# The first pair of groups 1 and 2 from SBUF, and their first products in two chains

## The chip, the cores and the metric

The kernel runs on one core of one Trainium2 chip. The metric is the device time of one execution in microseconds, the median of several runs.

## The reference

Three stages follow each other on 1536 tokens of width 512: an attention over a window of 16 and over summaries of blocks of 32 keys, a gated feed-forward layer (part 1 here), and a second feed-forward layer (part 2), which is all that the change names:

```python
def _moe2_ref(x, w_in, w_out) -> np.ndarray:
    h = x @ w_in
    g = h - np.tanh(h)
    return (g @ w_out).astype(np.float32)
```

In part 2 `x` is 1536 x 512, `w_in` 512 x 2048 and `w_out` 2048 x 512, all float32.

## The kernel before

Each float32 operand is split into a high half (a cast to fp32r, on ScalarE) and a low half (the difference, on VectorE or GpSimd), and each product is three matmuls: high by high, high by low, low by high (`mm3`, lines 838 to 840). The tokens form three groups of 512. The 2048 hidden columns of part 2 form 16 blocks of 128, taken two at a time: eight pairs n = 0 to 7.

For a pair, `h` is computed in seven block products instead of eight (`product(k, ...)`, k = 1 to 7, six matmuls of 256 columns each), here called the first products. Sums of the products on VectorE give the four quarters of `h`; then come tanh (ScalarE) and `h - tanh(h)` (VectorE). For groups 0 and 1 the result is split into `hh` and `hl` and multiplied by two blocks of `w_out` straight away: the second products, eight of a pair, three matmuls of 512 columns each, which add up in four `acc` banks over the eight pairs. Group 2 keeps its results in `wd[1]`, and its second products come last, again in seven block products (`last_seconds`), pair after pair.

The blocks of weights of the seven first products are sums of quarters of `w_in`. Group 0 makes them (`make`): sums in `sm`, split into the tiles `ih` and `il` in the large buffer `mix` (`eh` and `el` for pair 0), and stores them in DRAM as `ki{n}` (line 1305, two tiles of 1024 and two of 768 columns). Groups 1 and 2 load them (`fetch`) into `l0` and `l1`, places in `wd[0]`. In the same way group 0 stores the out-weights `kd`, group 1 loads them into `th` tiles (`fetch_d`, line 1341; two tiles), splits them (`direct_outs`, ScalarE at line 1361) and makes the block sums for the last stage (`make_values`), which are stored as `kv{n}` and loaded again by `place_values`.

The order of every engine is found by a planner in the kernel: each operation has an engine, a duration, the operations that it follows, the buffers that it takes and a due time; the planner starts what is ready, most urgent first, and emits the instructions in that order. Operations marked `flex` go to VectorE or GpSimd; the function `yields` decides whether GpSimd leaves one to VectorE. `LAG`, `EASE` and `RID` shift due times. All first products follow each other in one chain, `chain["first"]`; the pairs of groups 1 and 2 are visited as (1,0), (1,1), (2,0), (2,1), (1,2), (2,2), ... Transfers go through SyncE's queue in the planned order.

Of the kernel before, what the change touches and what calls it, by code (L numbers as in the profile page):

```python
# [59 lines left out]
LAND = 1.0  # L60
LAG = 4.0
EASE = 24.0
RID = 2.0
HOLD = 1.0
FRONT = 0.0
FAR = 4.0
# [29 lines left out]
class Plan:  # L96
# [25 lines left out]
    def order(self, filler=None, gap=0.0):  # L122
# [39 lines left out]
        def yields(o, eng, now):  # L162

            return eng == "pool" and free.get("dve", 0.0) <= now + 0.3 and any(
                q.late < o.late and q.port and q.ready <= now + 1e-9 and can(q, now) for _, _, q in ready.get("dve", [])
            )
# [115 lines left out]
def kernel(  # L282
# [1091 lines left out]
    def fetch(n):  # L1374
        weights = {}
        at = 0
        for i, ks in enumerate(turns):
            m = len(ks) * q
            w = [slot(f"l{i}"), slot(f"l{i}")]
            o = dma_both(m, True, w, [k[:, at:at + m] for k in keep_i[n]], *stored[n], *after_a, *made_o)  # L1380
            for i, k in enumerate(ks):
                weights[k] = (*w, i * q, *o)
            at += m
        return weights

    def make(n):
# [36 lines left out]
        for ks, pieces in zip(  # L1423
# [22 lines left out]
            m = len(ks) * q  # L1446
            store += dma_both(m, False, (wh, wl), [k[:, at:at + m] for k in keep_i[n]], *[o for p in done for o in p])
            for i, k in enumerate(ks):
                weights[k] = (wh, wl, i * q, *done[i])
            at += m  # L1450
        after_a.extend([o1, o2, o3, o4] + [o for p in weights.values() for o in p[3:]])
        stored[n] = store
        return direct_outs(n), weights

    direct = []
    halves_of = {}
    kept = lambda f: wd[1][:, f * 512:(f + 1) * 512]

    def pair(g, n, at, weights=None, period=PAIR):
# [11 lines left out]
        def product(k, m, out, opens, *after, closes=True):  # L1471
            wh, wl, w0, a, z = weights[k]
            h, l = operand[g][k]

            def run():
                for c in range(2):
                    s = slice(w0 + c * P, w0 + (c + 1) * P)
                    mm3(out(), wh[:, s], wl[:, s], h()[:, c], l()[:, c], opens and c == 0, closes and c == 1)

            count[0] += 1  # L1480
            o = pe(0.71, run, chain.get("first"), a, z, *ready[g][k], *after, slots=[m, wh, wl], due=at + count[0] * (PAIR if g < 2 else OPS * 0.715) / OPS)
            chain["first"] = o
            second_first.setdefault(g, []).append(o)
            return o
# [75 lines left out]

        opens, closes = n == 0, n == NF2 // 2 - 1
        nt = GROUPS[g][1]
# [6 lines left out]
        for j in (1, 0):  # L1569
            oh, ol, do = outs[j]  # L1570
            for i in range(nt):
# [7 lines left out]
                if not (closes and j == 0):  # L1579
                    continue  # L1580
                ob = slot("th")
                m = DM // 2
                a = act(0.27, lambda i=i, ob=ob: nc.scalar.copy(ob[:, :m], ps[i][:, :m]), after2, slots=[ps[i], ob], due=due + RID)
                z = dve(0.33, lambda i=i, ob=ob: nc.vector.tensor_copy(ob[:, m:], ps[i][:, m:]), after2, slots=[ps[i], ob], due=due + RID)
                t0_ = GROUPS[g][0]
# [18 lines left out]
    def make_values(n, d, outs, ld):  # L1604
# [4 lines left out]
        def put(ks, w, z):  # L1609
            m, c = len(ks) * q, CUTS[ks[0]]  # L1610
            for i, k in enumerate(ks):
                done[k] = *w, i * q, *z
            if n + 1 < NF2 // 2:
                stored_v.setdefault(n, []).extend(dma_both(m, False, w, [k[:, c:c + m] for k in keep_v[n]], *z, due=due))

        def item(ks, j, *after):
            w = slot("vh"), slot("vl")
            gate = [o for k in stored for o in stored[k]]
            put(ks, w, cut(lambda: d[j][:], lambda: w[0][:], lambda: w[1][:], 2 * q, chain.get("v"), *after, *gate, slots=[d[j], *w]))

# [15 lines left out]
    def h_forms(n):  # L1636
# [7 lines left out]
        def make_item(ks, src, m, *after):  # L1644
            hi, lo = slot("fh"), slot("fl")
            gate = second_first[1] if n == 0 and ks[0] < 3 else second_first[2]
            a, z = cut(src, lambda: hi[:, :m], lambda: lo[:, :m], m, chain.get("f"), *after, *gate, slots=[hi, lo])
            chain["f"] = a
            for i, k in enumerate(ks):
                forms[k] = hi, lo, i * q, a, z  # L1650
            return a, z
# [17 lines left out]
    def place_values(n):  # L1669

        if n + 1 == NF2 // 2:
            return
# [15 lines left out]
    def last_seconds(n, at, opens, closes):  # L1688
# [9 lines left out]
        for k in (1, 6, 7, 5, 2, 3, 4) if opens or closes else (1, 2, 4, 6, 7, 3, 5):  # L1698
            fh, fl, f0, *fo = forms[k]
            vh, vl, v0, *vo = values[n][k]  # L1700
            for a in range(2):
# [6 lines left out]
                count += 1  # L1708
                ss = [fh, fl, ps[k]] + ([vh, vl] if n + 1 == NF2 // 2 else [])
                after2 = pe(0.358, run, after2, *fo, *vo, slots=ss, due=at + count * 0.358)  # L1710
# [102 lines left out]
    prepare(2, at + PAIR)  # L1813
    line = [(g, 2 * k + j) for k in range(n_all // 2) for j in range(2) for g in (1, 2)]
    line[1], line[2] = line[2], line[1]
    weights = {}
    v_due = {n: at + 2 * n * 7.7 + EASE for n in range(n_all)}
    for i, (g, n) in enumerate(line):
        if n not in weights:
            weights[n] = fetch(n)  # L1820
        pair(g, n, at, weights[n], 2 * 7.75)
        at += 7.75
    at += 4.0
    for n in range(n_all):
        ends = last_seconds(n, at, not n, n + 1 == n_all)
        at += 2 * OPS * 0.358
# [111 lines left out]
```

## Time and profile before

| | |
|---|---|
| median of 3 runs | 652.35 us (648.78 to 653.7) |
| profiled execution | 650.38 us |
| its span in the trace | 648.5 us |
| TensorE busy | 631.1 us, 97% |
| VectorE, ScalarE, GpSimd busy | 523.6, 398.1, 107.6 us |
| DMA moved | 126.60 MB |
| group 0 of part 2 ends, groups 1 and 2 begin | at about 467 us |
| last stage of group 2 begins | at about 604 us |

The span is the stretch between the first and the last instruction of the profiled execution; 1.9 us of that execution lie outside it. A row names the line of the kernel, the engine and the tiles: `mid` and `bank` are PSUM banks, `mix` and `wd` are the two large buffers in SBUF that hold weights, `pad`, `hi`, `lo`, `rest` and `raw` are buffers that change their use from stage to stage. Where a text speaks of a matmul's distance from the next, the starts are compared, since ends overlap.

### The profile page before, as it was taken

How to read it: one execution, taken by the hardware profiler on the slowest of the kernel's cores; microseconds unless marked ns; L12 is line 12 of the kernel's file. 1: busy time of each engine (PE TensorE's matmuls, PEld its weight loads, DVE VectorE, ACT ScalarE, POOL GpSimd, SP SyncE). 2: the span in 40 equal slices, each digit the busy share in tenths (PEclk: the TensorE clock that was granted, in tenths of full speed). 3: DMA queues.
4: the chain of work that ended last, by engine and by line, in shares of the span. 5: the costliest groups of instructions: out<-in, count | busy, mean ns of one | idle time of the engine just before them, and what ended most of it. 6: DMA issues, size and time to landing. Idle time of an engine off the chain costs nothing.

```text
span 648.5 us, 11072 instructions
## 1 busy us (share of the span) xinstructions
PE 631.1 (97%) x3786; PEld 547.0 (84%) x3786; DVE 523.6 (81%) x1130; ACT 398.1 (61%) x829; POOL 107.6 (17%) x165
## 2 busy tenths in 40 slices
PE   7999999999999999999999999999899999999997
PEld 6997778789887888887888888898799999999996
DVE  5789878988699977888988989978666776668785
ACT  3996678878676545546656767665555555556441
POOL 2212333223042020221200002311020101110000
PEclk9999999999999999999999999999999999999999
DMA  9989457889300000235323255566477988898731
GB/s 333 354 267 330 157 158 239 287 296 307 102 1 1 33 1 1 97 130 172 124 64 130 116 187 206 206 241 231 156 267 227 351 282 295 269 375 343 266 142 66
DMA packets 46625, 126.60 MB, mean 195 GB/s; under 512 B 5560, under 2 KB 10600, under 8 KB 46568
## 3 DMA queue, kind: packets, MB, share of 16 engines
q1 hardware_dynamic: 46568, 125.89, 55.4%
q8 instruction: 30, 0.49, 0.3%
q14 instruction: 27, 0.22, 0.1%
HBM read 91.00 MB, written 34.87 MB: 194 GB/s over the span
## 4 chain that ended last, share of the span: by engine, by line
PE 80%; DMA 8%; DVE 7%; ACT 3%; issue 1%; SPq 0%; POOL 0%; DVEq 0%; ACTq 0%
PE bank L838 15%; PE bank L840 14%; PE bank L839 14%; PE mid L838 10%; PE mid L840 10%; PE mid L839 10%; PE bank L674 2%; DMA pad<-in_units_dram 2%; PE bank L580 2%; DMA hi<-in_w_dram 1%; PE bank L685 1%; DMA wd<-in_ksum_dram 1%; DMA wd<-in_units_dram 1%; DMA raw<-in_w_dram 1%; PE bank L631 1%
## 5 line engine op out<-in xcount | busy, mean ns | idle before, releaser
L838 PE MATMUL mid<-hi,mix 128*128 128x512 f32 (+1 forms) x160 | 63.6, 398 | 0.0
L840 PE MATMUL mid<-hi,mix 128*128 128x512 f32 (+1 forms) x160 | 59.5, 372 | 0.0
L840 PE MATMUL bank<-mix,hl 128*128 128x512 f32 x128 | 50.7, 396 | 0.0
L838 PE MATMUL bank<-mix,hh 128*128 128x512 f32 x128 | 50.6, 395 | 0.0
L838 PE MATMUL bank<-hh,mix 128*128 128x512 f32 (+1 forms) x128 | 50.0, 390 | 0.6 <-ACT hh L856 0.3
L839 PE MATMUL bank<-mix,hh 128*128 128x512 f32 x128 | 50.4, 394 | 0.0
L814 ACT CAST mix<-wd 128x512 fp32r<-128x512 f32 x66 | 40.3, 619 | 16.1 <-PE bank L839 12.1
L839 PE MATMUL bank<-hl,mix 128*128 128x512 f32 (+1 forms) x128 | 48.6, 379 | 1.0 <-DVE hl L859 1.0
L840 PE MATMUL bank<-hh,mix 128*128 128x512 f32 (+1 forms) x128 | 48.3, 378 | 0.0
L816 DVE TENSOR_TENSOR mix<-wd,mix 128x512 fp32r<-128x512 f32 x59 | 40.2, 683 | 8.6 <-ACT mix L814 8.5
L839 PE MATMUL mid<-lo,mix 128*128 128x512 f32 (+1 forms) x112 | 40.6, 363 | 0.0
L608 ACT ACTIVATE pad<-pad,st 128x184 f32<-128x184 f32 x88 | 32.3, 438 | 7.0 <-DVE st L594 6.9
L840 PE MATMUL mid<-pad,mix 128*128 128x256 f32 (+1 forms) x104 | 34.9, 335 | 1.5 <-DVE mix L1058 1.5
L838 PEld LDWEIGHTS mid<-hi,mix 128*128 128x128 f32 x160 | 30.1, 188 | 6.8 <-issue 2.7
L838 PE MATMUL mid<-pad,mix 128*128 128x256 f32 (+1 forms) x104 | 35.1, 337 | 0.2 <-ACT rest L1499 0.2
L840 PEld LDWEIGHTS mid<-hi,mix 128*128 128x128 f32 x160 | 30.1, 188 | 5.8
L839 PE MATMUL mid<-pad,mix 128*128 128x256 f32 (+1 forms) x104 | 34.8, 335 | 0.0
L1107 ACT COPY lo<-mid 128x512 f32<-128x512 f32 x36 | 21.0, 586 | 22.0 <-PE mid L840 21.5
L1110 DVE TENSOR_TENSOR lo<-lo,bank 128x512 f32<-128x512 f32 x36 | 24.5, 684 | 8.8 <-ACT lo L1107 6.4
L840 PE MATMUL bank<-pad,mix 128*128 128x512 f32 (+1 forms) x90 | 30.8, 343 | 0.0
L839 PE MATMUL bank<-pad,mix 128*128 128x512 f32 (+1 forms) x90 | 30.8, 342 | 0.0
L838 PE MATMUL bank<-pad,mix 128*128 128x512 f32 (+1 forms) x90 | 30.8, 342 | 0.0
(343 smaller groups left out, 2053.7 us busy)
## 6 DMA issues: line engine op xcount, KB each, us to landing
raw<-in_w_dram SPq DMA_DIRECT2D x38, 512.0 KB, 4.9
kv<-mix SPq DMA_DIRECT2D x42, 256.0 KB, 3.9
pad<-in_units_dram SPq DMA_DIRECT2D x19, 442.0 KB, 5.5
hi<-in_w_dram SPq DMA_DIRECT2D x16, 512.0 KB, 5.3
wd<-ki SPq DMA_DIRECT2D x16, 512.0 KB, 5.6
wd<-in_w_dram SPq DMA_DIRECT2D x14, 512.0 KB, 4.6
ki<-mix SPq DMA_DIRECT2D x14, 512.0 KB, 3.8
wd<-ki SPq DMA_DIRECT2D x16, 384.0 KB, 6.6
```

The lines of the kernel that those rows point to most:

```text
L580: nc.tensor.matmul(ps[e][:, j * SC:(j + 1) * SC], q[r, j], k[r, j], start=(j == 0), stop=(j == NP - 1), skip_group_check=True,)
L608: nc.scalar.activation(s, s, AF.Exp, bias=st[:, 0, h:h + 1], scale=-1.0)
L631: nc.tensor.transpose(pt[:, h * P:(h + 1) * P], sc[:, m0:m0 + P], ident)
L674: nc.tensor.matmul(av[:, h * (D + 1):(h + 1) * (D + 1)], ph[:, h * P:(h + 1) * P], v[:, h], start=(h == 0), stop=False, skip_group_check=True,
L685: nc.tensor.matmul(av[:, 2 * j * (D + 1):2 * (j + 1) * (D + 1)], ph[0:TAIL + 1, (4 + j) * P:(5 + j) * P], vtn[0:TAIL + 1, j].rearrange("p ...
L814: a = act(0.52, lambda c=c: nc.scalar.copy(wh[:, c], d[:, c]), dep, chain.get(tag), slots=[wh])
L816: on.tensor_tensor(wl[:, c], d[:, c], r32(wh[:, c]), ALU.subtract)
L838: nc.tensor.matmul(o, ah, bh, start=first, stop=False, skip_group_check=True)
L839: nc.tensor.matmul(o, ah, bl, start=False, stop=False, skip_group_check=True)
L840: nc.tensor.matmul(o, al, bh, start=False, stop=last, skip_group_check=True)
L1107: return act(0.52, lambda: nc.scalar.copy(u[m][:], mx[m][:]), *after, *free, slots=[u[m], mx[m]])
L1110: return dve(0.62, lambda: nc.vector.tensor_tensor(u[m][:], u[m][:], my[m][:], ALU.add), *after, slots=[u[m], my[m]])
```

## The change

Pair 7, which group 0 does last, is not stored: `make` hands its split weights on in `carried`, and groups 1 and 2 do pair 7 first, from `ih` and `il` in `mix`. The pairs then go in the order `TURN` = 7, 0, 1, ..., 6, group 1 and group 2 by turns, and the last stage in the same order. Each group has its own chain of first products. Pair 6 is now the one whose out-weight sums stay in SBUF; those of pair 7 are cut into free places of `l0` and `l1` and stored as `kv7`, and the load of pair 1 waits for that. Group 1's results leave through `tb` tiles. The look-ahead in `yields` goes from 0.3 to 2.0, `LAG` from 4 to 2, `EASE` from 24 to 16.

```diff
-LAG = 4.0
-EASE = 24.0
+LAG = 2.0
+EASE = 16.0
+YIELD = 2.0
+RIG = 2.0
+OFF = 2.0
+BOTH = 15.5
+TURN = [NF2 // 2 - 1, *range(NF2 // 2 - 1)]
...
         def yields(o, eng, now):
 
-            return eng == "pool" and free.get("dve", 0.0) <= now + 0.3 and any(
+            return eng == "pool" and free.get("dve", 0.0) <= now + YIELD and any(
...
-            o = dma_both(m, True, w, [k[:, at:at + m] for k in keep_i[n]], *stored[n], *after_a, *made_o)
+            o = dma_both(m, True, w, [k[:, at:at + m] for k in keep_i[n]], *stored[n], *after_a, *made_o, *(stored_v[TURN[0]] if n == TURN[2] else []))
...
-            store += dma_both(m, False, (wh, wl), [k[:, at:at + m] for k in keep_i[n]], *[o for p in done for o in p])
+            if n != TURN[0]:
+                store += dma_both(m, False, (wh, wl), [k[:, at:at + m] for k in keep_i[n]], *[o for p in done for o in p])
...
         stored[n] = store
+        if n == TURN[0]:
+            carried[n] = weights
         return direct_outs(n), weights
...
-            o = pe(0.71, run, chain.get("first"), a, z, *ready[g][k], *after, slots=[m, wh, wl], due=at + count[0] * (PAIR if g < 2 else OPS * 0.715) / OPS)
-            chain["first"] = o
+            o = pe(0.71, run, chain.get(("first", g)), a, z, *ready[g][k], *after, slots=[m, wh, wl], due=at + count[0] * (BOTH if g else PAIR) / OPS)
+            chain["first", g] = o
...
-        opens, closes = n == 0, n == NF2 // 2 - 1
+        opens, closes = (n == 0, n == NF2 // 2 - 1) if not g else (n == TURN[0], n == TURN[-1])
...
-                ob = slot("th")
+                ob = slot("tb" if g else "th")
...
         def item(ks, j, *after):
-            w = slot("vh"), slot("vl")
-            gate = [o for k in stored for o in stored[k]]
-            put(ks, w, cut(lambda: d[j][:], lambda: w[0][:], lambda: w[1][:], 2 * q, chain.get("v"), *after, *gate, slots=[d[j], *w]))
+            if n == TURN[0]:
+                w = [slot(f"l{j}") for i in range(2)]
+                gate = after_a + made_o
+            else:
+                w = [slot("vh"), slot("vl")]
+                gate = [o for g in (1, 2) for o in second_first[g][:OPS]] + [o for k in stored for o in stored[k]]
+            put(ks, w, cut(lambda: d[j][:], lambda: w[0][:, :2 * q], lambda: w[1][:, :2 * q], 2 * q, chain.get("v"), *after, *gate, slots=[d[j], *w]))
...
-    line = [(g, 2 * k + j) for k in range(n_all // 2) for j in range(2) for g in (1, 2)]
-    line[1], line[2] = line[2], line[1]
-    weights = {}
-    v_due = {n: at + 2 * n * 7.7 + EASE for n in range(n_all)}
+    line = [(g, TURN[2 * k + j]) for k in range(n_all // 2) for j in range(2) for g in (1, 2)]
+    weights = carried
+    v_due = {n: at + i * BOTH + EASE for i, n in enumerate(TURN)}
     for i, (g, n) in enumerate(line):
         if n not in weights:
             weights[n] = fetch(n)
-        pair(g, n, at, weights[n], 2 * 7.75)
-        at += 7.75
+        pair(g, n, at + (OFF if g == 2 else 0.0), weights[n], BOTH)
+        at += BOTH / 2
     at += 4.0
-    for n in range(n_all):
-        ends = last_seconds(n, at, not n, n + 1 == n_all)
+    for n in TURN:
+        ends = last_seconds(n, at, n == TURN[0], n == TURN[-1])
```

First place: TensorE where group 1 begins. `mid<-hi` is the first product k = 1 of group 1, the rows with `hh` and `hl` are second products of pair 6 of group 0; `wd` holds loaded blocks, `mix` those that group 0 made. Before:

```order
L838 MATMUL bank_78<-mix_89,hh_94 128x512
L839 MATMUL bank_78<-mix_89,hh_94 128x512
L840 MATMUL bank_78<-mix_89,hl_96 128x512
L838 MATMUL mid_81<-hi_0_61,wd_1_4142 128x256
L839 MATMUL mid_81<-hi_0_61,wd_1_4142 128x256
L840 MATMUL mid_81<-hi_0_61,wd_1_4142 128x256
```

Now:

```order
L843 MATMUL bank_76<-mix_89,hh_94 128x512
L844 MATMUL bank_76<-mix_89,hh_94 128x512
L845 MATMUL bank_76<-mix_89,hl_96 128x512
L843 MATMUL mid_81<-hi_0_61,mix_89 128x256
L844 MATMUL mid_81<-hi_0_61,mix_89 128x256
L845 MATMUL mid_81<-hi_0_61,mix_89 128x256
```

And where, in the new order, the first matmul on a loaded block comes (the rows with `pad` are first products of group 2):

```order
L843 MATMUL mid_82<-pad_1942,mix_89 128x256
L844 MATMUL mid_82<-pad_1942,mix_89 128x256
L845 MATMUL mid_82<-pad_1942,mix_89 128x256
L843 MATMUL mid_81<-hi_0_61,wd_1_4134 128x256
L844 MATMUL mid_81<-hi_0_61,wd_1_4134 128x256
L845 MATMUL mid_81<-hi_0_61,wd_1_4134 128x256
```

One second product more stands ahead of group 1, and its first product that reads `wd` stands 84 matmuls behind its first product of all.

Second place: VectorE at what was 208 us of the trace. L1058 (now L1063) makes low cuts of weights in `mix`, L1110 and L1135 (L1115 and L1140) add the two halves of a sum and apply the gate. Before:

```order
L1110 TENSOR_TENSOR lo_0_65<-lo_0_65,bank_78 128x512
L1110 TENSOR_TENSOR lo_0_65<-lo_0_65,bank_76 128x512
L1135 SCALAR_TENSOR_TENSOR th_91<-th_91,lo_0_65 128x512
L1058 TENSOR_TENSOR mix_89<-lo_0_65,mix_89 128x512
L1136 TENSOR_TENSOR th_91<-th_91,lo_0_65 128x512
L1058 TENSOR_TENSOR mix_89<-rest_71,mix_89 128x512
```

Now:

```order
L1115 TENSOR_TENSOR lo_0_65<-lo_0_65,bank_78 128x512
L1063 TENSOR_TENSOR mix_89<-lo_0_65,mix_89 128x512
L1115 TENSOR_TENSOR lo_0_65<-lo_0_65,bank_76 128x512
L1063 TENSOR_TENSOR mix_89<-rest_71,mix_89 128x512
L1140 SCALAR_TENSOR_TENSOR th_91<-th_91,lo_0_65 128x512
L1063 TENSOR_TENSOR mix_89<-lo_0_65,mix_89 128x512
L1141 TENSOR_TENSOR th_91<-th_91,lo_0_65 128x512
```

The cut `mix<-lo` that stood behind both sums and the gate now stands between the two sums, and a second cut stands ahead of the gate.

Third place: SyncE's queue in the middle of groups 1 and 2. `kv<-mix` stores sums of out-weights, `th<-kd` loads out-weights, `wd<-ki` loads blocks of first products. Before:

```order
L1305 DMA wd_1_4142<-ki_0_104 128x1024
L1305 DMA wd_1_4142<-ki_1_105 128x1024
L1305 DMA kv_0_132<-mix_89 128x512
L1305 DMA kv_1_133<-mix_89 128x512
L1305 DMA kv_0_132<-mix_89 128x512
L1305 DMA kv_1_133<-mix_89 128x512
L1341 DMA th_92<-kd_119 128x512
L1341 DMA th_91<-kd_118 128x512
L1305 DMA wd_1_4142<-ki_0_104 128x768
L1305 DMA wd_1_4142<-ki_1_105 128x768
```

Now:

```order
L1310 DMA wd_1_4134<-ki_0_102 128x768
L1310 DMA wd_1_4134<-ki_1_103 128x768
L1310 DMA kv_0_132<-mix_89 128x512
L1310 DMA kv_1_133<-mix_89 128x512
L1310 DMA kv_0_132<-mix_89 128x512
L1310 DMA kv_1_133<-mix_89 128x512
L1346 DMA th_91<-kd_119 128x512
L1346 DMA th_92<-kd_118 128x512
L1310 DMA wd_1_4134<-ki_0_104 128x1024
L1310 DMA wd_1_4134<-ki_1_105 128x1024
```

The two loads `th<-kd` stand behind the last two pairs of stores `kv` as before; the second half of the loads `wd<-ki` now stands ahead of these stores.

## Rows read from the trace of the kernel before

**Rows 1.** The page, part 1: busy us, share of the span and instructions.

```profile
...
PE 631.1 (97%) x3786; PEld 547.0 (84%) x3786; DVE 523.6 (81%) x1130; ACT 398.1 (61%) x829; POOL 107.6 (17%) x165
...
```

**Rows 2.** The page, part 4: the chain that ended last, by engine.

```profile
...
PE 80%; DMA 8%; DVE 7%; ACT 3%; issue 1%; SPq 0%; POOL 0%; DVEq 0%; ACTq 0%
...
```

**Rows 3.** Busy us by stretch (x instructions), then granted clock, DMA share, GB/s.

```profile
...
455.00:475.00 20.00, 17.68 (x102) 15.55 (x101) 12.23 (x22) 10.15 (x22) 1.22 (x1) 0.91 0.59 214
475.00:500.00 25.00, 25.00 (x169) 23.01 (x168) 17.42 (x33) 14.16 (x34) 5.09 (x5) 1.00 0.65 225
500.00:525.00 25.00, 24.54 (x171) 22.79 (x171) 17.24 (x37) 13.94 (x31) 1.86 (x2) 1.00 0.94 337
525.00:600.00 75.00, 75.00 (x515) 69.50 (x514) 52.81 (x107) 41.71 (x92) 8.12 (x9) 1.00 0.85 310
...
```

**Rows 4.** TensorE's waits, whole span: us in total, times, longest.

```profile
...
PE mid L840 <- DVE mix L1058: 1.5, 1, 1.5
...
PE bank L839 <- DVE hl L859: 1.0, 2, 0.7
...
```

**Rows 5.** TensorE's waits from 440 to 648 us.

```profile
...
PE mid L838 <- DMA wd<-ki: 1.5, 1, 1.5
PE mid L840 <- DMA wd<-ki: 0.8, 1, 0.8
PE mid L838 <- ACT lo L1499: 0.5, 1, 0.5
PE bank L838 <- ACT th L1583: 0.3, 1, 0.3
```

**Rows 6.** Timeline of SyncE's queue at 465 us: start, us, what.

```profile
...
464.97 3.70 SPq L1305 DMA_DIRECT2D wd<-ki  x8
...
```

**Rows 7.** Timeline of TensorE at the same place.

```profile
...
466.39 0.39 PE L839 MATMUL bank<-mix,hh 128*128 128x512 f32 x1
466.62 0.39 PE L840 MATMUL bank<-mix,hl 128*128 128x512 f32 x1
468.54 0.39 PE L838 MATMUL mid<-hi,wd 128*128 128x256 f32 x1 [1.53 <-DMA wd<-ki]
...
469.83 0.49 PE L840 MATMUL mid<-hi,wd 128*128 128x256 f32 x1 [0.78 <-DMA wd<-ki]
...
```

**Rows 8.** One microsecond behind it, columns as in rows 3.

```profile
...
470.00:471.00 1.00, 1.00 (x5) 1.00 (x6) 0.00 (x0) 0.00 (x1) 0.00 (x0) 0.50 1.04 414
...
```

**Rows 9.** Groups of VectorE, then ScalarE, 480 to 600 us: busy, mean ns, idle before.

```profile
...
L1557 DVE TENSOR_TENSOR hl<-lo,hh 128x512 fp32r<-128x512 f32 x16 | 11.5, 717 | 3.9 <-ACT hh L1556 3.9
...
L1492 DVE TENSOR_TENSOR lo<-lo,bank 128x256 f32<-128x256 f32 x15 | 6.2, 416 | 2.6 <-ACT lo L1499 2.6
...
L1538 DVE TENSOR_TENSOR wd<-lo,wd 128x512 f32<-128x512 f32 x7 | 4.9, 694 | 4.8 <-ACT wd L1534 4.7
...
L1534 ACT ACTIVATE wd<-lo 128x512 f32<-128x512 f32 x16 | 10.2, 634 | 3.5 <-DVE lo L1492 3.3
L1556 ACT CAST hh<-lo 128x512 fp32r<-128x512 f32 x16 | 9.9, 621 | 4.4 <-PE bank L839 3.4 <-DVE lo L1538 0.9
...
```

**Rows 10.** Timelines of GpSimd, then VectorE, at 231 us.

```profile
...
231.27 0.75 POOL L1026 TENSOR_TENSOR rest<-wd 128x256 f32<-128x256 f32 x1 [21.72 <-DVE mix L1058]
...
230.51 0.69 DVE L1058 TENSOR_TENSOR mix<-rest,mix 128x512 fp32r<-128x512 f32 x1
...
233.64 1.23 DVE L1058 TENSOR_TENSOR mix<-lo,mix 128x512 fp32r<-128x512 f32 x1
...
```

**Rows 11.** Timelines of TensorE, VectorE and GpSimd at 208 us.

```profile
...
210.16 0.50 PE L840 MATMUL mid<-pad,mix 128*128 128x512 f32 x1 [1.54 <-DVE mix L1058]
...
208.35 1.75 DVE L1058 TENSOR_TENSOR mix<-lo,mix 128x512 fp32r<-128x512 f32 x1
...
206.58 2.98 POOL L816 TENSOR_TENSOR mix<-wd,mix 128x512 fp32r<-128x512 f32 x2
```

**Rows 12.** DMA issues, whole span: count, KB each, median us to landing.

```profile
...
wd<-ki SPq DMA_DIRECT2D x16, 384.0 KB, 6.6
...
th<-kd SPq DMA_DIRECT2D x16, 256.0 KB, 5.2
...
```

More of the change, by code (lines that the diff above doesn't have):

```diff
@@ L1452, in make @@
         stored[n] = store
+        if n == TURN[0]:
+            carried[n] = weights
         return direct_outs(n), weights
+    carried = {}
     direct = []
@@ L1580, in pair @@
                     continue
-                ob = slot("th")
+                ob = slot("tb" if g else "th")
                 m = DM // 2
-                a = act(0.27, lambda i=i, ob=ob: nc.scalar.copy(ob[:, :m], ps[i][:, :m]), after2, slots=[ps[i], ob], due=due + RID)
-                z = dve(0.33, lambda i=i, ob=ob: nc.vector.tensor_copy(ob[:, m:], ps[i][:, m:]), after2, slots=[ps[i], ob], due=due + RID)
+                a = act(0.27, lambda i=i, ob=ob: nc.scalar.copy(ob[:, :m], ps[i][:, :m]), after2, slots=[ps[i], ob], due=due + (RIG if g else RID))
+                z = dve(0.33, lambda i=i, ob=ob: nc.vector.tensor_copy(ob[:, m:], ps[i][:, m:]), after2, slots=[ps[i], ob], due=due + (RIG if g else RID))
                 t0_ = GROUPS[g][0]
@@ L1612, in put @@
                 done[k] = *w, i * q, *z
-            if n + 1 < NF2 // 2:
+            if n != TURN[-1]:
                 stored_v.setdefault(n, []).extend(dma_both(m, False, w, [k[:, c:c + m] for k in keep_v[n]], *z, due=due))
         def item(ks, j, *after):
-            w = slot("vh"), slot("vl")
-            gate = [o for k in stored for o in stored[k]]
-            put(ks, w, cut(lambda: d[j][:], lambda: w[0][:], lambda: w[1][:], 2 * q, chain.get("v"), *after, *gate, slots=[d[j], *w]))
+            if n == TURN[0]:
[5 more added lines that the diff above has]
+            put(ks, w, cut(lambda: d[j][:], lambda: w[0][:, :2 * q], lambda: w[1][:, :2 * q], 2 * q, chain.get("v"), *after, *gate, slots=[d[j], *w]))
         def tt(out, x, z, *after):
@@ L1645, in make_item @@
             hi, lo = slot("fh"), slot("fl")
-            gate = second_first[1] if n == 0 and ks[0] < 3 else second_first[2]
+            gate = second_first[1] if n == TURN[0] and ks[0] < 3 else second_first[2]
             a, z = cut(src, lambda: hi[:, :m], lambda: lo[:, :m], m, chain.get("f"), *after, *gate, slots=[hi, lo])
@@ L1669, in place_values @@
     def place_values(n):
-        if n + 1 == NF2 // 2:
+        if n == TURN[-1]:
             return
@@ L1708, in last_seconds @@
                 count += 1
-                ss = [fh, fl, ps[k]] + ([vh, vl] if n + 1 == NF2 // 2 else [])
+                ss = [fh, fl, ps[k]] + ([vh, vl] if n == TURN[-1] else [])
                 after2 = pe(0.358, run, after2, *fo, *vo, slots=ss, due=at + count * 0.358)
```

## The prediction

> **What bounds the kernel now.** I read the page's first section first: TensorE is busy 631.1 of 648.5 us, 97%, and no other engine is above 84% [rows 1]. Then the chain that ended last: four fifths of it are matmuls, the rest is the start-up's transfers and a few waits [rows 2]. The number of matmuls does not change, so only three things can move the time: the places where TensorE stands still, its clock, and the first 50 us, which the change leaves in order. Third, I read the span in stretches [rows 3]: in 525 to 600 us TensorE is busy 75.00 of 75, in 475 to 500 us 25.00 of 25; in 455 to 475 us only 17.68 of 20, and of the four only there is the granted clock below 1 (0.91). That is where group 0 of part 2 ends and group 1 begins. Last, the list of TensorE's waits, over the whole span [rows 4] and from 440 us on [rows 5]: behind 440 us there are four waits, 3.1 us in all, and 2.3 of these are for `wd<-ki`, the reload of weight blocks.
>
> **The junction.** Group 1 begins with the blocks of pair 0, which come back from DRAM into `l0`/`l1`. Eight loads are issued at 464.97 us, over 3.70 us [rows 6]; they can't go earlier, because these tiles are read until then by the cuts of pair 7. TensorE's last second product for which it needs nothing starts at 466.62; the next matmul, the first on a loaded block, starts at 468.54, and another waits until 469.83 [rows 7]. Matmuls of 512 columns start 0.23 us apart (466.39, 466.62), those of 256 half that. So TensorE loses 468.54 - 466.62 - 0.23 = 1.69 and 469.83 - 468.54 - 2 x 0.12 = 1.05, together 2.74 us. Behind it the engine runs on 0.50 of its clock [rows 8], the lower of its two levels (1.2 GHz against 2.4), in each of the three microseconds from 470 to 473 and in a part of the next: at least 3 x 0.50 = 1.5 us lost, and at most what the mean of 0.91 over 20 us gives, 1.8 [rows 3]; I take 1.7. Together 4.4 us.
>
> What the change puts there: in the order of TensorE the first product of group 1 reads `mix`, the blocks of pair 7 that group 0 has just used, and needs no load. The first product that needs one (pair 0, group 1) stands behind ten first products (six matmuls of 256 columns, 0.71 us each) and eight second ones (three of 512, 0.69 each) of the new order, which is 12.6 us after 467.6, at about 480.2 us. Its four loads are issued as before, since their tiles come free at the same point, and the last of the eight that was waited for had landed 4.9 us after the first issue (464.97 to 469.83); the four of pair 1 now stand behind stores of `kv`, and are needed 10 us later still. So 10 us lie between landing and use, and this wait goes. With it goes the slower clock, if nothing else lets TensorE stand. What is late next is VectorE: the second products of pair 7 of group 0 wait for their low halves (`hl`), which are ready about 0.2 to 0.4 us ahead of their place in the order; I put 0.2 us on that. **-4.4, +0.2.**
>
> **The two chains.** With `chain["first", g]` the products of groups 1 and 2 alternate. Per pair and per 15.5 us the work is the same (14 first, 8 second products). What shrinks is the distance from the last first product of group 1 that feeds the tanh (k = 4) to the first second product: 5 first and 1 second product, 5 x 0.71 + 0.69 = 4.25 us, for six of eight pairs (4.9 us or more in the other two); before, 13 steps, 9.2 us, for four of them. In that distance lie the sum on VectorE (0.42), tanh on ScalarE (0.63), the difference (0.69), the cast (0.62) and the low half (0.72), 3.08 us by the mean of each group [rows 9]; with the other work that stands between them in the engines' orders I find some 0.25 us to spare. A wait arises if a GpSimd instruction falls beside one of the three VectorE steps. The nearest row: a 128x256 subtraction of GpSimd takes 0.75 us where it is alone, and of four VectorE instructions beside four of these the most stretched took 1.23 instead of 0.68 us [rows 10], 0.55 more. GpSimd has 5 + 2 + 9 = 16 instructions in the 125 us from 475 on [rows 3], two per pair; the three steps are 1.82 us, and with 0.75 for the other's length they are open to a hit for 2.57 of 15.5 us, twice: a third of the pairs. Seven pairs x 1/3 x (0.55 - 0.25) = **+0.7**. The bounds are 0 and 7 x 2 x 0.55 = 7.7 us; nothing speaks for the upper one, since the two would have to hit in every pair.
>
> The Trainium skill ("SBUF — State Buffer", section "SBUF: two separate sides") says of the ports that GpSimd and VectorE share that they are locked for a whole instruction and that the other engine stands fully blocked. By it each hit would cost the whole instruction of GpSimd, an estimated 0.75 us instead of 0.55, and the term would be 1.2 us instead of 0.7. The rows above show less than that, and I keep theirs.
>
> **What YIELD moves.** GpSimd now leaves an instruction to VectorE if that is free within 2 us and has something more urgent of the shared kind; 21 instructions go from GpSimd to VectorE, and from some 55 us on the order of every engine differs in places. A subtraction of 256 columns costs VectorE about 0.34 us from start to start, and on GpSimd it stretches VectorE's own by up to the 0.55 above: even, or slightly better. TensorE waits for neither as a rule. One place counts: at 208 us the third matmul of a block waits 1.54 us for the low cut `mix` of VectorE, which took 1.75 instead of 0.68 us, beside two cuts on GpSimd, 2.98 us together [rows 11]. In the new order this cut stands two places earlier, ahead of the second sum and the silu, and the two cuts of GpSimd stand behind it on VectorE: **-1.5**. Three more have weaker reasons: the shorter of the two waits for `hl` (1.0 - 0.7 = 0.3 us, at 303 us [rows 4]; two VectorE instructions that stood before it now stand behind), 0.5 us at 517 us (ScalarE's copy `lo` [rows 5]; the order there is new) and 0.3 us at 606 us (the evacuation `th` [rows 5], which now goes through another tile). With what TensorE loses from start to start beside each wait they are 1.6 us; I take half: **-0.8**. The order from 55 to 180 us is new too; TensorE loses about 0.1 us per 20 there now, so there is little to gain and up to 1 us to lose or, by the waits for GpSimd that start-up has, win; I take 0 and put 1 us in the range.
>
> **What else it drops.** Four stores and four reloads of pair 7, 2 x 512 + 2 x 384 KB either way: 3.6 MB of 126.6. In 500 to 525 us the queues are 0.94 busy [rows 3], so this can help, but no wait of TensorE hangs on it there. The results of group 1 leave through `tb`; 8 evacuations as before, 0 us. The last stage takes pair 7 first: its second block (k = 6) needs a cut that is ready 0.1 to 0.2 us ahead of it, two products later; **+0.2**.
>
> **Sum.** -4.4 + 0.2 + 0.7 - 1.5 - 0.8 + 0.2 = -5.6 us. The profiled execution took 650.38 us; it would take 644.8. The median of the runs, 652.35, is 2.0 us above that execution, and the runs lie from 648.78 to 653.7; the sum is taken off the median: **646.8 us**, 0.86% faster.
>
> **Rivals.**
> *All waits behind 55 us go.* 4.4 + 1.5 + 1.6, and about 3 us of smaller ones spread over the rest (0.1 per 20 us, and 1.3 us at 390 to 396 us): 10.5 us, 641.8. For it: each place that I looked at has a new order. Against: the way from tanh to second product has become shorter, and a new order makes its own waits. Half way, 643.5.
> *The loads of `kd` come late.* Group 1's out-weights come through two `th` tiles, 256 KB each, 5.2 us from issue to landing in the median [rows 12]. In the queue of SyncE they stand behind the stores of `kv`, as before; but in the new order of ScalarE the cast that takes them stands between the two casts `hh`, which the second products wait for, and ScalarE comes to it 3 to 5 us after the issue. Up to a landing of 4.5 us nothing waits for long enough to matter, since TensorE has some 1.5 us to spare behind that cast; at the median ScalarE stands for up to 2.2 us and TensorE for 0.7; at 6.6 us, the median of the 384 KB loads of `wd` in the same queue [rows 12], 2.1. Seven pairs x 2.1 = 14.7 us against the 6.7 of gains (4.4 + 1.5 + 0.8), 660.3; if the clock falls each time as at 470 us, up to 665. The time comes out above 652.35 if each pair loses 1.0 us, from a landing of 5.5 us in every pair on. For it: 500 to 525 us is crowded (0.94). Against: traffic falls, the `th` tiles have two slots, and before ScalarE waited for these loads in only some pairs.
> *The junction's wait only moves.* If `hl` or the products' sums on VectorE come late, since VectorE must finish group 0 and prepare group 2 there, 2 of the 4.4 us come back and the rest of the sum stays small: 650.
> That the change doesn't do what it says can be excluded for the loads: the queue of the changed kernel has no store or load of pair 7's blocks.
>
> **How the numbers follow.** Near the forecast (643.5 to 649): 0.52. More waits gone (640 to 643.5): 0.17. Moved or half given back (649 to 653): 0.22. `kd` late in most pairs (653 to 665): 0.09. A measurement of this kernel can tell about 1%, 6.5 us, from no change: faster by more is below 645.8, which is the second case and 0.2 of the first, 0.37 in all; slower by more is above 658.9, the upper part of the last, 0.06; the rest is 0.57. The range for 8 in 10 leaves a tenth at each end: 642.0 to 652.5.
>
> **What would show it.** In the profile after: no wait of TensorE for `wd<-ki`, a granted clock of 1.00 at 465 to 475 us, no wait for `mix` at 208 us; a list of waits behind 440 us below 2 us in all, of which `hl` is the longest. If `hl` or `lo` of part 2 stands there with a wait in every pair, the chain is too short; if ScalarE's idle time before the cast of `th` is over 2 us per pair, it is `kd`. I am wrong if the new order from 55 to 400 us makes waits of more than 2 us, which no row of before can tell.

## The result and the profile after

The changed kernel takes 643.47 us in the median of 4 runs (641.57 to 645.42), the kernel before 652.15 us in the runs beside it (648.78 to 653.7): a ratio of 0.9874, interval 0.9824 to 0.9924 (ratios are taken over all runs, so they are not quite the quotient of the two medians). Timed a second time it was 640.96 against 650.7 us, 0.9852 (0.9826 to 0.9877). So the gain is 8 to 10 us, not the 5.6 of the sum. The profiled execution took 642.69 us, its span is 640.9 us.

First the page's part 1, which answers to [rows 1]:

```profile
...
PE 627.5 (98%) x3786; PEld 544.3 (85%) x3786; DVE 522.2 (81%) x1151; ACT 394.8 (62%) x829; POOL 80.2 (13%) x144
...
```

TensorE is busy 3.6 us less with the same 3786 matmuls, and the span is 7.6 us shorter. GpSimd is busy 27 us less, and VectorE no more than before, though it took over 21 instructions. Added up over the trace, VectorE's instructions that run beside one of GpSimd's took 12 us longer than the median of their shape, in the kernel before 22 us: so what it took over was about made up for by less stretching.

Then the stretches of [rows 3], same columns (busy time and count of TensorE, its weight loads, VectorE, ScalarE and GpSimd; granted clock; DMA share; GB/s):

```profile
...
455.00:475.00 20.00, 20.00 (x128) 18.12 (x127) 15.45 (x29) 12.38 (x27) 2.32 (x3) 1.00 0.39 132
475.00:500.00 25.00, 25.00 (x176) 23.09 (x175) 16.99 (x34) 13.17 (x31) 2.81 (x3) 1.00 0.80 274
500.00:525.00 25.00, 25.00 (x178) 23.38 (x177) 17.75 (x38) 14.06 (x32) 1.07 (x1) 1.00 0.94 324
525.00:600.00 75.00, 74.64 (x514) 69.11 (x513) 51.13 (x110) 37.82 (x88) 3.29 (x3) 1.00 0.77 270
...
```

In 455 to 475 us TensorE is now busy all the time, 128 matmuls where 102 stood, and the clock is 1.00 instead of 0.91. The DMA share there is 0.39 instead of 0.59.

TensorE's waits, some of them over the whole span (of [rows 4], `mix` is gone and `hl` down to 0.2 us) and all behind 440 us, where [rows 5] had four:

```profile
...
PE bank L843 <- DVE lo L1501: 0.7, 1, 0.7
...
PE mid L843 <- ACT hh L861: 0.3, 1, 0.3
...
PE mid L844 <- DVE hl L864: 0.2, 1, 0.2
...
```

```profile
...
PE mid L843 <- ACT rest L1508: 0.4, 1, 0.4
```

One wait of 0.4 us is left of the 3.1. At the junction, SyncE's queue and TensorE:

```profile
...
462.39 1.75 SPq L1310 DMA_DIRECT2D wd<-ki  x4
...
464.25 0.39 PE L843 MATMUL bank<-mix,hh 128*128 128x512 f32 x1
...
464.93 0.28 PE L843 MATMUL mid<-hi,mix 128*128 128x256 f32 x1
...
477.56 0.28 PE L843 MATMUL mid<-hi,wd 128*128 128x256 f32 x1
...
```

The four loads of pair 0 are issued at 462.39, and the first product that reads one starts at 477.56, 15.2 us later. The first product of group 1 (464.93) follows the second product before it (464.25, the first of three matmuls 0.23 apart) without a gap: it reads `mix`. And at 208 us (now 206), VectorE, then TensorE:

```profile
...
204.28 0.69 DVE L1115 TENSOR_TENSOR lo<-lo,bank 128x512 f32<-128x512 f32 x1 [0.50 <-PE bank L845]
204.88 0.68 DVE L1063 TENSOR_TENSOR mix<-lo,mix 128x512 fp32r<-128x512 f32 x1
205.68 0.69 DVE L1115 TENSOR_TENSOR lo<-lo,bank 128x512 f32<-128x512 f32 x1
...
207.12 0.40 PE L844 MATMUL mid<-pad,mix 128*128 128x512 f32 x1
207.36 0.40 PE L845 MATMUL mid<-pad,mix 128*128 128x512 f32 x1
...
```

The low cut `mix<-lo` (204.88) stands between the two sums, takes 0.68 us instead of the 1.75 of [rows 11], and the two matmuls stand 0.24 us apart.

Where TensorE lost time can be added up over the whole trace: the distance from each matmul's start to the next one's, less 0.231 us for 512 columns and 0.1185 for 256 (and one median for the other shapes, which stand in the first 182 us; there the differences between profiles count, not the level). Two profiles of each kernel (the second ones are among the experiments), in us:

```
stretch (of before)        before   before, 2nd   after   after, 2nd
start, 0 to 180 us           16.1       14.2       15.0      15.0
180 to 300 us                 2.7        2.7        0.9       0.9
300 to 400 us                 2.3        2.7        2.5       1.2
400 to 460 us                 0.2        0.1        0.1       0.2
junction, 460 to 480 us       4.5        3.1       -0.1       0.0
480 to 600 us                 1.5        3.0        1.2       0.9
600 us to the end             0.8        0.8        0.3       0.3
sum                          27.8       26.6       20.0      18.4
```

The sums, taken before rounding, differ as the spans do (648.5, 647.2, 640.9, 639.3 us). Behind 180 us the change saves 7.8 us in the mean of the two pairs; the start changes by 2 us from one execution to the next of the same kernel.

### The profile page after: what moved, and what is told of

It reads as the page before. It is cut to its first block, busy times and chain, and to the rows that moved or that the text cites. A ratio compares the mean times of both kernels' runs of the same rounds, so it can differ in the third digit from the quotient of the medians.

```text
span 640.9 us, 11000 instructions
## 1 busy us (share of the span) xinstructions
PE 627.5 (98%) x3786; PEld 544.3 (85%) x3786; DVE 522.2 (81%) x1151; ACT 394.8 (62%) x829; POOL 80.2 (13%) x144
## 4 chain that ended last, share of the span: by engine, by line
PE 78%; DMA 9%; DVE 5%; ACT 5%; issue 1%; SPq 1%; POOL 0%; DVEq 0%; ACTq 0%
PE bank L843 14%; PE bank L845 14%; PE bank L844 14%; PE mid L843 10%; PE mid L844 9%; PE mid L845 9%; DMA raw<-in_w_dram 3%; PE bank L679 2%; DMA wd<-in_ksum_dram 2%; PE bank L585 2%; DMA pad<-in_units_dram 1%; PE bank L690 1%; DMA th<-kd 1%; DMA wd<-in_units_dram 1%; PE bank L636 1%
## 5 line engine op out<-in xcount | busy, mean ns | idle before, releaser
L843 PE MATMUL mid<-hi,mix 128*128 128x512 f32 (+1 forms) x166 | 66.0, 398 | 0.0
L845 PE MATMUL mid<-hi,mix 128*128 128x512 f32 (+1 forms) x166 | 61.2, 369 | 0.0
L821 DVE TENSOR_TENSOR mix<-wd,mix 128x512 fp32r<-128x512 f32 x60 | 41.5, 696 | 12.1 <-ACT mix L819 11.9
L843 PE MATMUL mid<-pad,mix 128*128 128x256 f32 (+1 forms) x114 | 37.9, 332 | 0.2 <-ACT rest L1508 0.2
L844 PE MATMUL mid<-pad,mix 128*128 128x256 f32 (+1 forms) x114 | 37.6, 330 | 0.0
L845 PE MATMUL mid<-pad,mix 128*128 128x256 f32 (+1 forms) x114 | 37.6, 329 | 0.0
L843 PEld LDWEIGHTS mid<-hi,mix 128*128 128x128 f32 x166 | 31.3, 188 | 6.9 <-issue 2.7
L845 PEld LDWEIGHTS mid<-hi,mix 128*128 128x128 f32 x166 | 31.2, 188 | 5.8
L1115 DVE TENSOR_TENSOR lo<-lo,bank 128x512 f32<-128x512 f32 x36 | 24.6, 686 | 10.8 <-ACT lo L1112 7.3
L845 PE MATMUL bank<-pad,mix 128*128 128x512 f32 (+1 forms) x96 | 32.6, 339 | 0.0
L844 PE MATMUL bank<-pad,mix 128*128 128x512 f32 (+1 forms) x96 | 32.5, 339 | 0.0
L843 PE MATMUL bank<-pad,mix 128*128 128x512 f32 (+1 forms) x96 | 32.5, 338 | 0.0
```

Of the source, the lines that this page charges most:

```text
L821: on.tensor_tensor(wl[:, c], d[:, c], r32(wh[:, c]), ALU.subtract)
L843: nc.tensor.matmul(o, ah, bh, start=first, stop=False, skip_group_check=True)
L844: nc.tensor.matmul(o, ah, bl, start=False, stop=False, skip_group_check=True)
L845: nc.tensor.matmul(o, al, bh, start=False, stop=last, skip_group_check=True)
L1115: return dve(0.62, lambda: nc.vector.tensor_tensor(u[m][:], u[m][:], my[m][:], ALU.add), *after, slots=[u[m], my[m]])
```

## The experiments

Two theories stood against each other. **Separate places:** the blocks in SBUF take the junction's wait, YIELD the ones at 208 and 303 us, the new due times and order of pairs the rest. **Chains:** it is the two chains side by side that give TensorE other work, and the blocks alone would not have done it. A third asked how much of it all is the spread from run to run.

**The changed kernel again, and the kernel before again**, each for a second profile.

> The changed kernel once more, with a second profile. If the 0.9 us that TensorE lost less in the first 60 us (9.9 against 10.8 us beyond the matmuls' spacing) belongs to the execution and not to the change, this profile shows a value between 9.5 and 11 there, and the other places (208, 303, 467, 517, 606 us) the same within 0.3 us as the first. If each place moves from execution to execution, they differ by 0.5 us and more.

Measured: 0.9852 (above), span 639.3 us. From 180 us on the places are the same within 0.3 us, except for one wait at 378 us (0.9 us in the first profile, none in the second) and one at 560 us (0.5 us, then 0.2). The first 60 us lost 9.0 us, below the stated 9.5: the start varies more than that.

> The kernel before once more, for a second profile. The first was taken of an execution of 650.38 us, 1.1 us below the median of 20 runs (651.46). If the places of the sum belong to the order, 4.4 us are lost at the junction again, 1.7 at 208 us, 0.5 at 303, 0.6 at 517 and 0.4 at 606 us, each within 0.2 us, and what differs lies in the start and up to 180 us. Rival: waits of half a microsecond move from execution to execution, so that 303, 517 and 606 us prove nothing.

Measured: 651.02 us against 651.5, ratio 0.9999 (0.9965 to 1.0033). The five places are there again: 1.70 us at 206, 0.52 at 301, 0.69 at 515, 0.45 at 604 us, and the junction, so they belong to the order. The rival is half right all the same: 0.4 us at 380 and 0.5 us at 501 and at 584 us stand in this profile alone, and 480 to 600 us lost 3.0 us instead of 1.5. The junction lost less, though. Its two waits on TensorE, and the stretch around them:

```profile
...
466.94 0.39 PE L838 MATMUL mid<-hi,wd 128*128 128x256 f32 x1 [1.45 <-DMA wd<-ki]
...
468.44 0.39 PE L840 MATMUL mid<-hi,wd 128*128 128x256 f32 x1 [1.00 <-DMA wd<-ki]
...
455.00:475.00 20.00, 17.55 (x110) 15.42 (x110) 13.13 (x23) 10.54 (x23) 0.74 (x1) 1.00 0.60 211
...
```

The two waits are as long as in [rows 7], 1.45 and 1.00 us behind the semaphores and 2.8 us from start to start, but the clock stayed at 1.00: 3.1 us lost and not 4.5.

**YIELD, taken back and alone.**

```diff
-YIELD = 2.0
+YIELD = 0.3
```

> The changed kernel with YIELD set back to 0.3, nothing else. Theory of separate places: the waits of the stage from 180 to 310 us come back, 1.5 to 2.2 us, the junction at 467 us stays without a wait, so the time lies 1.5 to 2.5 us above the changed kernel, ratio to before 0.990 to 0.992. Rival, that the order of VectorE and GpSimd counts for nothing: same time as the changed kernel, 0.987. Rival, that YIELD counts most, by freeing VectorE everywhere: 4 us or more come back.

Measured: 644.68 us, 0.9893 (0.9867 to 0.9919). TensorE's waits from 180 to 310 us:

```profile
...
PE mid L845 <- DVE mix L1063: 1.5, 1, 1.5
PE mid L843 <- ACT hh L861: 0.5, 1, 0.5
PE bank L844 <- DVE hl L864: 0.4, 1, 0.4
```

The 1.5 us for `mix` are back, with two others for `hh` and `hl`; behind 440 us no wait at all is listed. Against the changed kernel in the same runs (0.9852) that is 0.4%, 2.7 us, a little above the stated 1.5 to 2.5; the two intervals just overlap.

```diff
-            return eng == "pool" and free.get("dve", 0.0) <= now + 0.3 and any(
+            return eng == "pool" and free.get("dve", 0.0) <= now + 2.0 and any(
```

> The kernel before with the look-ahead of 2.0 in the choice between GpSimd and VectorE, nothing else. Separate places: no wait at 208 us, 4.4 us lost at the junction as before, ratio 0.995 to 0.998. If YIELD counts most: 0.993 or less and a shorter loss at the junction.

Measured: 649.54 us, 0.9969 (0.9949 to 0.9988); no wait from 180 to 310 us, the junction as before (4.4 us). YIELD is worth some 2 us, by these two places and by this ratio.

**One chain instead of two, with the blocks in SBUF.**

```diff
-            o = pe(0.71, run, chain.get(("first", g)), a, z, *ready[g][k], ...
-            chain["first", g] = o
+            o = pe(0.71, run, chain.get("first"), a, z, *ready[g][k], ...
+            chain["first"] = o
```

> The changed kernel with one chain of first products for groups 1 and 2 together; pair 7 first and from SBUF, as changed. If the SBUF blocks alone remove the wait of the junction: TensorE waits for no load there (0 to 0.5 us lost at 455 to 475 us against 4.4 before) and the time is within 2 us of the changed kernel, ratio 0.987 to 0.990. Rival, that the wait went because two chains side by side give TensorE other products to do: 2 us and more are lost at the junction or at the first products on loaded blocks, ratio 0.992 or above.

Measured: 643.87 us, 0.988 (0.9854 to 0.9906). No wait for a load; behind 440 us the longest one is

```profile
...
PE mid L843 <- ACT rest L1508: 1.0, 1, 1.0
...
```

at 494 us, with 0.4 us more at 480 us: 1.9 us lost from 460 to 500 us against 0.1. The blocks alone take the junction's wait away. With one chain TensorE waits for ScalarE's copy `rest`, 1 to 2 us lost; the runs alone can't tell this kernel from the changed one (0.988 and 0.9852 beside each other). Over all profiles it shows in 480 to 600 us: those with two chains lost 0.5 to 1.6 us there (`after`, `again`, `yield_back`, `reload`, `low_half_twice`, `start_filled`, `start_bare`), those with one chain 1.5 to 4.8 (`before`, `before_again`, `yield_alone`, `fill`, `one_chain`, `rest_alone`). Four of these six have the old order of pairs as well.

**Two chains, with the reload.**

```diff
-TURN = [NF2 // 2 - 1, *range(NF2 // 2 - 1)]
+TURN = list(range(NF2 // 2))
...
-            if n != TURN[0]:
+            if True:
                 store += dma_both(m, False, (wh, wl), ...
-        if n == TURN[0]:
-            carried[n] = weights
```

> The changed kernel without the carried pair: group 0 stores pair 7 again, groups 1 and 2 go from pair 0 to pair 7 and load every block, with two chains side by side and all other numbers as changed. If the SBUF blocks remove the wait: TensorE waits for the reload at the junction again, 2 to 3 us, runs at half clock behind it for another 1.5 us or so, and the ratio to before is 0.993 to 0.998. If the two chains remove it, it is 0.987 to 0.990 and no wait for a load shows.

Measured: 644.99 us, 0.9913 (0.9881 to 0.9945). TensorE at the junction, and the two microseconds behind it:

```profile
...
463.93 0.39 PE L843 MATMUL mid<-hi,wd 128*128 128x256 f32 x1 [0.95 <-DMA wd<-ki]
...
465.19 0.39 PE L845 MATMUL mid<-hi,wd 128*128 128x256 f32 x1 [0.75 <-DMA wd<-ki]
...
466.00:468.00 2.00, 2.00 (x12) 2.00 (x11) 1.11 (x2) 1.89 (x4) 0.00 (x0) 0.50 0.86 281
...
```

Both waits are back, 0.95 and 0.75 us long, with the clock at 0.50 behind them: 3.8 us lost. The cut leaves out the edits that follow from this, on the loads and on the out-weight sums of the first pair. Against the changed kernel (0.9852 and 0.9874) that is 2.5 to 4 us. The chains theory falls.

**The wait filled, in the kernel before.**

```diff
+            if (g, n) == (1, 0):
+                def fill():
+                    h = operand[1][1][0]
+                    for i in range(22):
+                        nc.tensor.matmul(al(), h()[:, 0, 0:P], h()[:, 0], start=True, stop=True, skip_group_check=True)
+
+                chain["first"] = pe(0.1, fill, chain.get("first"), direct[-10], *ready[1][1], slots=[m1], due=at)
             p1 = product(1, m1, al, True, closes=False)
```

> The kernel before with 22 matmuls of 256 columns on idle data put where TensorE waits for the reload (their results are overwritten; 22 x 0.12 = 2.6 us). If the half clock behind the wait is a consequence of standing still: the granted clock stays at 1.00 from 466 to 474 us, the time between the last matmul before the wait and full speed is 2.7 us and no longer 4.4, and the whole kernel is 1.5 to 1.7 us faster than before (0.997 to 0.998, hardly to be told from 1 by the time alone). Rival, that the slow clock comes from what else runs there, the transfers above all: the clock falls to 0.50 all the same.

Measured: 649.45 us, 0.9974 (0.9945 to 1.0002). The 22 matmuls (468.29, to the next start 2.63 us), what is left of the wait, and a microsecond behind it:

```profile
...
468.29 2.79 PE L1505 MATMUL mid<-hi 128*128 128x256 f32 x22
470.92 0.28 PE L838 MATMUL mid<-hi,wd 128*128 128x256 f32 x1
...
471.55 0.38 PE L840 MATMUL mid<-hi,wd 128*128 128x256 f32 x1 [0.24 <-DMA wd<-ki]
...
472.00:473.00 1.00, 1.00 (x8) 0.87 (x7) 0.00 (x0) 0.67 (x2) 0.00 (x0) 1.00 1.03 392
...
```

The transfers run as before (DMA share 1.03) and the clock is 1.00. The time can't be told from no change, since the interval takes in 1. And this profile cannot prove alone that the filling did it, since the kernel before kept its clock in its second profile without it. Over all profiles: of five that wait at the junction (`before`, `before_again`, `yield_alone`, `reload`, `rest_alone`) the clock fell in three; in the nine without that wait (filled, or no load needed) it stayed. The length of the waits doesn't sort the five: behind 0.95 and 0.75 us in `reload` the clock fell, behind 1.45 and 1.00 us in `before_again` it did not. The transfers alone do not cause it: they run in `before_again`, `rest_alone` and `fill` too.

**The chain from tanh to second product, made longer.**

```diff
+            def low(j=j):
+                for i in range(2 if g and j else 1):
+                    nc.vector.tensor_tensor(hl[j][:], th[j][:], r32(hh[j][:]), ALU.subtract)
+
-            l = dve(0.62, lambda j=j: nc.vector.tensor_tensor(hl[j][:], th[j][:], r32(hh[j][:]), ALU.subtract), h, ...
+            l = dve(0.62, low, h, ...
```

> The changed kernel with the first low half of each pair of group 1 (the one that the first second product of the pair waits for) written twice, 0.6 us more on VectorE in the chain from tanh to second product; nothing else moves. By the step of the prediction that this chain has 0.25 us to spare, TensorE waits about 0.35 us in each of the eight pairs, 2 to 3 us in all, and the list of waits shows hl. Rival, that the engines' orders leave 0.8 us or more: no waits for hl, 0 to 0.5 us in all.

Measured: 642.67 us, 0.9862 (0.9832 to 0.9892). TensorE's waits for `hl` from 455 us on:

```profile
...
PE bank L845 <- DVE hl L1568: 0.2, 1, 0.2
```

A low half written once more takes 0.73 us from start to start, not 0.6, and the slack hides it but for these 0.2 us.

> As low_half_twice, but written three times, 1.2 us more. In the second profile of the changed kernel the low half of group 1 was ready 0.7 to 0.8 us ahead of the third matmul of the second product, the first one that reads it, in six of eight pairs. By that, 1.2 us more cost 0.4 to 0.5 us in each, 3 to 4 us in all, with hl in the list of waits; time 2 to 4 us above the changed kernel. If the slack were the 0.25 us of the prediction, 0.6 us more would have cost 2.8 us (it cost no more than 1.2), and 1.2 more would cost 7.

Measured: 648.71 us, 0.9964 (0.9946 to 0.9982), 5 to 8 us above the changed kernel. The same list:

```profile
...
PE bank L845 <- DVE hl L1568: 4.6, 8, 1.0
...
```

Written three times the low half takes 1.45 us more, not 1.2. Each of the eight pairs waits 0.6 us for it, and from start to start these eight places lose 6.1 us, so the cost is twice what was expected. The time by itself would also fit the 7 us that were stated for a slack of 0.25 us; the list doesn't, as by that slack each pair would wait 1.2 us, and neither does the run before. The second profile of the unchanged chain shows the slack, VectorE's low half and the second product that reads it:

```profile
...
539.68 0.69 DVE L1566 TENSOR_TENSOR hl<-lo,hh 128x512 fp32r<-128x512 f32 x1 [1.15 <-ACT hh L1565]
...
540.71 0.40 PE L843 MATMUL bank<-mix,hh 128*128 128x512 f32 x1
...
541.17 0.40 PE L845 MATMUL bank<-mix,hl 128*128 128x512 f32 x1
...
```

The low half is done at 540.37; the second product starts at 540.71, but only its third matmul, at 541.17, reads `hl`. So there are 0.80 us to spare here, 0.7 to 0.8 in six of the eight pairs (1.1 and 0.4 in the other two). Both lists fit that: 0.73 us more just fit in, and of 1.45 some 0.65 are left over.

**The rest alone:** reload, one chain and YIELD 0.3 together.

> The changed kernel without its three large parts: pair 7 stored and loaded again and the pairs from 0 to 7, one chain of first products, YIELD 0.3. What is left: the due times, the order of the groups' pairs by turns from the first pair on, and the results of group 1 through tb. By the sum of places: 4 us lost at the junction, the wait at 208 us there, the waits at 517 and 606 us gone, ratio 0.996 to 0.999. Rival, that these two went with the chains or with the carried pair: they show here too, and the ratio is 1.000 or above.

Measured: 649.94 us, 0.9967 (0.9948 to 0.9986). The waits at 517 and 606 us are gone, the one at 208 us is there, and from 440 us on stand

```profile
...
PE mid L843 <- ACT rest L1506: 1.3, 1, 1.3
PE bank L845 <- DMA wd<-ki: 1.0, 1, 1.0
PE mid L843 <- DMA wd<-ki: 0.8, 1, 0.8
PE mid L845 <- DMA wd<-ki: 0.8, 1, 0.8
...
```

the junction's loads with 3.4 us lost, and a new wait for `rest` at 499 us; in 480 to 600 us it loses 4.8 us. This profile saves nothing over the kernel before (span 648.8 us), while the runs say 2 us; where these are could not be found in the one execution.

**The start.** In the profiles of `fill` and `yield_alone` the clock also fell, to 0.50 between 12 and 21 us, behind a wait of TensorE for GpSimd. Two runs asked whether that makes the spread of the runs:

```diff
-WARM = 12
+WARM = 17
...
+    calls = [0]
+
     def keep_up(n=1):
-        for _ in range(n):
+        calls[0] += 1
+        for _ in range(n + (5 if calls[0] == 10 else 0)):
```

> The changed kernel with 5 more idle 128-column products in each of the two places of the start where TensorE stands for 1.2 to 2.1 us (at 6 and at 10 us). Theory: where that standing is long enough in an execution, the clock falls to half for some microseconds (it did in two of nine profiles, at 12 to 18 us, and cost 1 to 2 us there); filled, the clock stays at 1.00 there in every execution, the runs lie closer together, and the median is 0 to 1.5 us below the changed kernel. Rival, that the spread of the runs comes from elsewhere: no difference.

Measured: 641.3 us (640.59 to 643.6), 0.9858 (0.9831 to 0.9885): no difference from the changed kernel, though TensorE does not stand there any more. In the profile the idle matmuls reach to the next product:

```profile
...
8.54 3.17 PE L1851 MATMUL mid<-idle 128*128 128x128 f32 x26
11.69 1.17 PE L585 MATMUL bank<-wd 64*128 64x184 f32 x8
...
```

And the other way, with `range(0 if 3 <= calls[0] <= 10 else n)` and WARM as it was:

> The changed kernel without the eight idle products in the second of these places, so that TensorE stands for 3.4 us there instead of 1.3 to 2.1. Theory: the clock falls to half behind it in every execution, 1 to 3 us lost, ratio to the changed kernel above 1.002. Rival, the clock there does not depend on standing still: no change.

Measured: 641.47 us (640.28 to 642.57), 0.9847 (0.9823 to 0.9872): not slower at all, although the wait and the slow clock are there:

```profile
...
11.79 1.70 PE L585 MATMUL bank<-wd 64*128 64x184 f32 x8 [3.31 <-POOL wd L557]
...
12.00:14.00 2.00, 2.00 (x11) 1.59 (x11) 1.97 (x12) 1.38 (x4) 0.24 (x3) 0.57 0.99 384
14.00:16.00 2.00, 2.00 (x13) 1.97 (x12) 1.92 (x8) 1.43 (x4) 0.32 (x3) 0.58 1.07 400
16.00:18.00 2.00, 2.00 (x21) 2.00 (x20) 1.42 (x5) 1.87 (x5) 0.65 (x3) 1.00 1.04 415
...
```

3.3 us of standing and four microseconds at 0.57 and 0.58. The 600th matmul of the feed-forward layers starts at 222.2 us, in the second profile of the changed kernel at 222.0: the 2.1 us that `start_bare` is behind at 96 us are found again by then. What holds that stretch in both kernels no run shows; that it is the transfers and the other engines is a guess. Neither run bears out the theory of the spread (640.59 to 643.6 us filled, 640.28 to 642.57 bare, 639.91 to 643.84 the changed kernel), though with four to six runs each a small difference would not be seen.

## Why the prediction was right, point by point

**The junction (-4.4, +0.2).** Right in place and mechanism: the wait went with the blocks in SBUF (`one_chain`, `reload`), and the new order lost nothing there, so the 0.2 for `hl` did not come. The size was taken from one profile: the 2.7 us of waiting are certain (2.7 and 2.8 us in two profiles), the 1.7 us of half clock belong to some executions only: the two profiles of before differ by 1.4 us at this place, and the clock fell in three of the five profiles with the wait. That -4.4 came out is in so far luck.

**YIELD (-1.5, and a part of -0.8).** Right: 1.7 us at 208 us, and by `yield_back` and `yield_alone` the two waits in 180 to 310 us go and come with this one number.

**The three weaker ones (-0.8 taken of 1.6).** All three went, so this term was sized at half its value; but other waits of half a microsecond come and go in these stretches, in the changed kernel one at 560 us. 303 us is YIELD's. 517 and 606 us went with the rest of the new order; they are absent in `rest_alone`, `one_chain` and `reload`, and present in `yield_alone`.

**The two chains (+0.7).** The step that failed, in size and sign. The prediction found some 0.25 us to spare up to the begin of the second product, and there are 0.34 in the pair shown above; but the low half is first read by the third matmul, 0.46 us later. With 0.7 to 0.8 us to spare in most pairs a hit of 0.55 us makes no wait. One such hit stands in the profile after, GpSimd beside the difference (0.69 us alone) of the first pair of group 1:

```profile
...
475.94 0.74 POOL L1635 TENSOR_TENSOR th<-th 128x256 f32<-128x256 f32 x1
...
476.04 1.19 DVE L1547 TENSOR_TENSOR lo<-lo,wd 128x512 f32<-128x512 f32 x1 [0.36 <-ACT wd L1543]
...
```

The low half behind it is done 0.84 us ahead of its matmul even so, and TensorE does not wait. `yield_back`, with 8 GpSimd instructions from 475 to 600 us, has no wait behind 440 us either. The term also counted too many hits: it took the 16 GpSimd instructions of before, while the new look-ahead leaves 7 (3, 1 and 3 in the stretches above). The price that the prediction worked out from the Trainium skill ("SBUF — State Buffer", section "SBUF: two separate sides"), an estimated 0.75 us a hit, can't be told here from the 0.55 of the rows, since the slack of most pairs covers both. Against one chain in the same order of pairs the two chains gained: 1.9 us in the trace, 0.3% by the runs, though the intervals overlap.

**The last stage (+0.2) and the order from 55 to 180 us (0).** No wait at the begin of the last stage; from 600 us on 0.3 us are lost instead of 0.8. The first 180 us lost 15.0 us in both profiles, between the two values of before (14.2, 16.1): no change that can be told.

**Sum.** In the first pair of profiles: -4.5 (junction), -1.8 (180 to 300 us), -0.3 (480 to 600), -0.5 (the end), +0.3 (300 to 400) and -1.1 in the start, which scatters as much: the span is 7.6 us shorter, where the sum said 5.6. Behind 180 us alone the first pair saves 6.7 us and the second 9.0; the prediction's gains with the weak waits in full and none of its losses, 4.4 + 1.5 + 1.6 = 7.5 us, lie between. By this the missing 2 us are the other half of the weak waits (0.8), the chains' +0.7 and the two +0.2. The runs gain 8 to 10 us, up to 2 more than the profiles; where these lie is open. The forecast of 646.8 us was 3 us too high: 643.47 is the lower end of its nearest case (643.5 to 649).

**The rivals.** "All waits behind 55 us go" came nearest in the number (half way from 646.8 to 641.8 is 644.3, not the 643.5 that the prediction wrote). Not in full, though: of the waits at 390 and 396 us, 1.2 us are left in the first profile and 1.0 in the second. `kd` late: it is not. ScalarE's idle time for these loads and the median landing (5.2 us in [rows 12]) are

```profile
...
  DMA th<-kd: 2.9, 4
...
```

```profile
...
th<-kd SPq DMA_DIRECT2D x16, 256.0 KB, 4.3
...
```

2.9 us in four waits from 455 to 600 us, where before had 4.4 in five. "The wait only moves": it did not; the first wait behind the junction is at 560 us, 0.4 us long.

## What to carry to other kernels

Where a stage begins with data that the stage before has just thrown out, start it with what is still on the chip: the reload then has the length of that first piece to land, here 15 us for loads that took 4.0 and 5.6 us from issue to landing. The slack of an operand counts to the instruction that reads it, not to the begin of the group that it belongs to: half a microsecond of difference turned a cost into none. And a second profile of the same kernel is worth its time: here the five waits that stood in both went with the order, while others of half a microsecond, and the slower clock behind a wait, were in one profile and not in the next.

## What the runs showed that was not expected

The granted clock behind the same two waits (2.7 and 2.8 us of standing still in all) fell to 0.50 (1.2 GHz) for three microseconds in the first profile of the kernel before and stayed at 1.00 (2.4 GHz) in the second. And a slow clock in the start, 0.57 over four microseconds behind 3.3 us of standing, cost the whole kernel nothing that the runs could tell (0.9847 against 0.9852).
